# Local attention and a gated MLP on one core: the output product of the last batch by seven block products

## The chip, the core and the metric

One NeuronCore of a Trainium2 chip runs the whole program. Its engines are TensorE (PE in the rows, with its weight loads as PEld), VectorE (DVE), ScalarE (ACT), GpSimd (POOL) and SyncE (SP, which here issues DMAs). They run side by side, each in the order of its own instruction queue, and wait for each other by semaphores. The metric is device time in microseconds. Every time here is of the program of one launch.

## The reference

Four batches of 768 tokens, 8 heads of 64. Attention looks at chunks of 32 tokens, each with 16 tokens to its left, 8 to its right and 8 memory tokens. Its output x (768 x 512 per batch) goes through a gated MLP; the products are what TensorE spends its time on:

```python
h = np.maximum(x @ w_in, 0.0)                       # 512 -> 1024
u, v = h[..., :512], h[..., 512:]
v_n = (v - mean(v)) / np.sqrt(var(v) + 1e-06)
v_s = np.einsum('ts,bsd->btd', w_spatial, v_n) + b_spatial[None, :, None]
gated = u * v_s
out = (gated @ w_out).astype(np.float32)            # 512 -> 512
```

## The kernel before

Every fp32 operand of the MLP is kept as two rounded parts, a high one (an ACT copy) and a low one (value minus high part, on DVE or POOL), and a product is three matmuls: high by high, low by high, high by low. A group of matmuls sums into one PSUM tile `f`. A block is 128 rows by 512, 384 or 256 columns.

The program runs over the batches. Per batch there are `ffn_v` (v, six groups of 12 matmuls of 512 columns), `ffn_u` (u, eight groups of 12 of 384), the spatial product (`spatial`, L1061 and after) and the output product (`ffn_o`). The attention of the next batch is laid between the matmuls of the present one: for each block of 128 tokens one burst of 64 small matmuls (scores of one block, values of the block before), and between two bursts a softmax chain over DVE, ACT and POOL.

In the last batch there is no attention left to lay between. There the spatial product is already done by Strassen: `strassen` makes seven products of half size, P2, P1, P6, P5, P3, P7, P4, of 18 matmuls of 384 columns each (L1236). Their right-hand sides are sums of blocks of v (`forms`) and of w_spatial (`w_forms`, L1201 for the sums, L1210 and L1212 for the two parts). After a product DVE adds the PSUM tile to the bias, or to what was kept (L1294); a finished quarter is multiplied by u on POOL (L1275) and split again into its parts g (ACT L1280, DVE L1284). Then `ffn_o` makes the output: six tiles of 128 tokens, each 12 matmuls of 512 columns (four blocks of g by three). The last tile is made as two halves of 256 columns. ACT copies each tile out (L1399) and SP stores it (L1401).

What runs when is not in the order of the code. `Plan` collects all operations with their engine, a cost, what they read and write and a rank; `order` then sets every engine's queue by simulating them, and the instructions are issued in that order. POOL and DVE share a way to SBUF, and the plan keeps them apart there: while any POOL operation runs, no DVE operation marked `port` is placed, and the other way round. `ORDER` is a table of corrections by operation number (a shift of the rank, a bonus in waiting, an engine), which here covers operations 0 to 429 only:

```python
if e == "POOL" or e == "DVE" and ops[n][11]:
    late = max(late, free["port"])
```

Of the kernel before, what the change touches and what calls it, by code (L numbers as in the profile page):

```python
# [8 lines left out]
F32 = mybir.dt.float32  # L9
# [111 lines left out]
}  # L121
# [86 lines left out]
class Plan:  # L208
# [13 lines left out]
    def op(self, eng, us, fn, r=(), w=(), rank=0.0, moves=0.0, tail=0.0, after=None, count=0, port=False):  # L222
        n = len(self.ops)
        wait = 0.0
# [25 lines left out]
        return n  # L250

    def order(self):
# [20 lines left out]
        while len(out) < len(ops):  # L273
            best = None
            for e, ns in waiting.items():
                pick, lead = None, None
                for n in ns:
# [15 lines left out]
                    if e == "POOL" or e == "DVE" and ops[n][11]:  # L293
                        late = max(late, free["port"])
# [23 lines left out]
            if e == "POOL" or e == "DVE" and port:  # L318
                free["port"] = t + us
# [41 lines left out]
def tile_chunked_attention_gmlp(  # L361
# [508 lines left out]
    def place(i, rank):  # L870
        j = i - 1

        def go(e, c):
            if c == 0:
                alloc("xs", j, [P, T, UC, CH], F32)
# [339 lines left out]

    def strassen(b):
# [8 lines left out]
        def product(name, form, piece_, banks, first, reads=((), ())):  # L1225
            begun = []
            prev = t_.get("product", last["u"])
            for j in range(2):
                cols = slice(j * P, (j + 1) * P)
                for s in range(NQ):  # L1230
                    def go(j=j, s=s, cols=cols):
# [9 lines left out]
                               *(x for f in ("B11", "B21") for y in range(NQ) for x in piece_keys(f, y) if name == "P2" and s == 0)],  # L1241
                            w=[("f", banks[j], name, s)], rank=1e4 + seq[0], tail=0.25, after=prev, count=6)
# [18 lines left out]
        def out_of(hf, d, rank, start_, more=()):  # L1261
# [10 lines left out]

            def mult():
                a = t_["st", s_]
                nc.gpsimd.tensor_tensor(a, a, t_["u", i], op=ALU.mult)  # L1275

            def high():
                if not g_place(i):
                    t_["g", i] = alloc("big", big, [P, 1024], U32).bitcast(F32R).rearrange("p (s n) -> p s n", s=2)
                nc.scalar.copy(g_of(i)[0][:, 0:HT], t_["st", s_])  # L1280

            def low():
                h, l_ = g_of(i)
                nc.vector.tensor_tensor(l_[:, 0:HT], t_["st", s_], h[:, 0:HT].bitcast(F32), op=ALU.subtract)  # L1284
            op("POOL", 1.05, mult, r=[("u", i)], w=[k_], rank=rank)
            op("ACT", act(HT), high, r=[k_], w=[gh], rank=rank)
            op("DVE", dve(HT), low, r=[k_, gh], w=[gl], rank=rank)
# [32 lines left out]
        last[b, 0] = last[b, 1]  # L1320
        for hf in range(2):
            for t in range(HU):
                ffn_o(b, hf, t, 2 if hf == 1 and t == HU - 1 else 1)
# [18 lines left out]
    def spatial(b, hf, d):  # L1342
# [33 lines left out]
        op("POOL", 1.05, mult, r=[("u", i)], w=[k_], rank=rank)  # L1376
        op("ACT", act(HT), high, r=[k_], w=[("big", big, "h")], rank=rank)
        op("DVE", dve(HT), low, r=[k_, ("big", big, "h")], w=[("big", big, "l")], rank=rank)
# [26 lines left out]
    def from_f64(name, dst, src_, rank, load_rank, over=(), pieces=1, gate=None, stage=None):  # L1405
# [58 lines left out]
        def convert():  # L1464
# [11 lines left out]
            op("POOL", 1.27, add, r=[(big[0], big, "r")], w=[zk], rank=rank + LATER)  # L1476
# [17 lines left out]
    def w_sp_part(t, rank, load_rank):  # L1494
# [13 lines left out]
        op("POOL", pool_(S), low, r=[("big", big), ("wsp", t, "h")], w=[wl_key(t) + ("l",), *(early_keys() if t < 3 else ())], rank=rank)  # L1508
# [22 lines left out]
    for b in range(B):  # L1531
# [17 lines left out]
        if b == B - 1:  # L1549
            w_forms()  # L1550
            strassen(b)
# [50 lines left out]
```

## Time and profile before

| | us |
|---|---|
| median of 3 runs | 373.35 (373.32 to 374.25) |
| the profiled execution, as a whole | 372.5 |
| its span, first to last instruction | 370.7 |
| PE busy | 353.7 (95%) |
| DVE, ACT, POOL busy | 226.4, 259.5, 162.9 |
| the seven spatial products of the last batch | 328.66 to 350.69 |
| the output product of the last batch | 350.69 to 367.37 |

An engine's busy time counts matmuls with modelled, overlapping ends, so a stretch of matmuls is read by the distance from one start to the next. The output product ends 3.3 us before the span does; what lies between is the last copy and the last store.

### The profile page before, as it was taken

To read this page: it belongs to the slowest core of one execution; us is meant where nothing else is said; L and a number is where in the kernel's file an instruction comes from. 1 tells how busy PE (TensorE), PEld (TensorE's weight loads), DVE (VectorE), ACT (ScalarE), POOL (GpSimd) and SP (SyncE) were. 2 spreads that over 40 slices of the span, in tenths; PEclk is the share of its full clock that TensorE was granted. 3 is DMA by queue.
4 is the path that set the end of the run, shared out by engine and by line. 5 is a ranking of instruction groups with operands and counts; after the bars stand their busy time and mean duration, and the time that the engine had idled before them with its cause. 6 is when DMAs were issued, how large, how long until landed. Compare 5 with 4: busy or idle time off the path is not lost.

```text
span 370.7 us, 11379 instructions
## 1 busy us (share of the span) xinstructions
PE 353.7 (95%) x4710; PEld 316.7 (85%) x4710; DVE 226.4 (61%) x445; ACT 259.5 (70%) x678; POOL 162.9 (44%) x255
## 2 busy tenths in 40 slices
PE   3659999999999999999999999999999999999996
PEld 3437988999899898899899889899899889899985
DVE  2797878977556376647448476555538477784610
ACT  5688898863596697887886787967886876551222
POOL 3776674653454241432543330543533563724600
PEclk9998999999999999999999999999999999999999
DMA  6999847881105271061025272071030230200013
GB/s 219 288 317 243 294 110 205 235 256 54 55 34 175 93 166 51 3 224 51 2 88 175 87 143 76 6 226 33 20 131 2 87 127 3 87 0 2 0 58 113
DMA packets 30108, 42.08 MB, mean 114 GB/s; under 512 B 5288, under 2 KB 23400, under 8 KB 30056
## 3 DMA queue, kind: packets, MB, share of 16 engines
q1 hardware_dynamic: 29832, 41.26, 36.4%
q8 instruction: 37, 0.61, 0.7%
q14 instruction: 15, 0.12, 0.1%
q10 hardware_dynamic: 224, 0.08, 0.1%
HBM read 35.05 MB, written 6.29 MB: 112 GB/s over the span
## 4 chain that ended last, share of the span: by engine, by line
PE 91%; DMA 4%; DVE 2%; ACT 1%; issue 1%; SPq 0%
PE f L1061 75%; PE sx L789 8%; PE f L1236 6%; DMA big<-in_moe_w_in_dram 4%; PE xt L1005 1%; PE pt L978 1%; SPq L512 0%; ACT vmain L737 0%; DVE win_l L1463 0%; DVE stage_z L1445 0%; PE f L789 0%; DVE st L1451 0%; DVE xs L859 0%; DVE p L907 0%; ACT st L1435 0%
## 5 line engine op out<-in xcount | busy, mean ns | idle before, releaser
L1061 PE MATMUL f<-x,win_h 128*128 128x384 f32 x256 | 72.7, 342 | 0.0
L879 ACT COPY xs<-sx 32x128 f32<-32x128 f32 x240 | 61.5, 256 | 3.4 <-PE sx L789 0.6
L1061 PE MATMUL f<-win_h,x 128*128 128x512 f32 x192 | 63.3, 411 | 0.0
L1061 PE MATMUL f<-wout,big 128*128 128x512 f32 x252 | 62.7, 392 | 0.0
L1061 PEld LDWEIGHTS f<-wout,big 128*128 128x128 f32 x252 | 46.7, 188 | 8.8
L1061 PEld LDWEIGHTS f<-x,win_h 128*128 128x128 f32 x256 | 47.0, 188 | 1.4
L1061 PE MATMUL f<-x,win_l 128*128 128x384 f32 x128 | 43.3, 338 | 0.0
L1366 POOL TENSOR_TENSOR st<-st,u 128x384 f32<-128x384 f32 x24 | 25.4, 1065 | 39.0 <-DVE st L1362 34.4
L1061 PEld LDWEIGHTS f<-win_h,x 128*128 128x128 f32 x192 | 35.7, 192 | 7.5 <-DVE x L1015 0.9
L486 ACT COPY pT<-p 32x128 f32<-32x128 f32 x128 | 37.9, 296 | 2.5 <-POOL p L958 1.0
L1061 PE MATMUL f<-win_l,x 128*128 128x512 f32 x96 | 38.7, 403 | 0.0
L1061 PE MATMUL f<-wsp_h,vb 128*128 128x384 f32 x144 | 37.5, 341 | 0.0
L958 POOL TENSOR_TENSOR p<-p,rec 128x512 f32<-128x512 f32 x15 | 16.0, 1064 | 48.0 <-DVE rec L935 48.0
L1061 PE MATMUL f<-wsp_h,va 128*128 128x384 f32 x144 | 36.9, 337 | 0.0
L486 POOL COPY pT<-p 32x128 f32<-32x128 f32 x112 | 33.7, 301 | 5.0
L1107 POOL TENSOR_TENSOR rstd<-ve,mhalf 128x1 f32<-128x1 f32 x24 | 15.9, 664 | 38.3 <-DVE ve L1103 20.5
L922 ACT ACTIVATE p<-p 128x512 f32<-128x512 f32 x24 | 15.1, 629 | 21.4 <-DVE p L907 21.3
L1399 ACT COPY st<-f 128x512 f32<-128x512 f32 (+1 forms) x25 | 13.9, 571 | 20.4 <-PE f L1061 17.2
L1061 PEld LDWEIGHTS f<-wsp_h,va 128*128 128x128 f32 x144 | 26.1, 188 | 0.6
L1061 PEld LDWEIGHTS f<-wsp_h,vb 128*128 128x128 f32 x144 | 25.7, 188 | 1.0
L1099 DVE BATCH_NORM_STATS2 stats<-st 128x6 f32<-128x512 f32 x24 | 16.6, 691 | 14.8 <-ACT st L1095 14.6
L1061 PEld LDWEIGHTS f<-x,win_l 128*128 128x128 f32 x128 | 24.1, 188 | 0.9
(164 smaller groups left out, 721.5 us busy)
## 6 DMA issues: line engine op xcount, KB each, us to landing
out_dram<-st SPq DMA_DIRECT2D x23, 256.0 KB
k<-in_k_dram SPq DMA_DIRECT2D x7, 800.0 KB
q<-in_q_dram SPq DMA_DIRECT2D x7, 768.0 KB
vmain<-in_v_dram SPq DMA_DIRECT2D x38, 128.0 KB
big<-in_moe_w_spatial_dram SPq DMA_DIRECT2D x12, 384.0 KB
vmain<-in_v_dram SPq DMA_DIRECT2D x37, 96.0 KB
big<-in_moe_w_in_dram SPq DMA_DIRECT2D x4, 512.0 KB
stage_w<-in_moe_w_in_dram SPq DMA_DIRECT2D x4, 512.0 KB
```

The costliest lines, as they stand in the source:

```text
L486: return (nc.scalar.copy if e == "ACT" else nc.gpsimd.tensor_copy)(o, a).ins
L789: nc.tensor.matmul(o, w_, m, start=start, stop=True, skip_group_check=True)
L879: last_ = (nc.scalar.copy if e == "ACT" else nc.vector.tensor_copy)(o, a).ins
L922: nc.scalar.activation(p3, p3, AF.Exp, scale=scale)
L958: (nc.vector if e == "DVE" else nc.gpsimd).tensor_tensor(p3, p3, rec, op=ALU.mult)
L978: nc.tensor.transpose(a[:, t], p[:, t], ident)
L1061: return [nc.tensor.matmul(o, ll if x == 1 else lh, rl if x == 2 else rh, start=x == j == 0, stop=j == len(pairs) - 1 and x == (single[-1] ...
L1099: nc.vector.bn_stats(stats, t_["st", s])
L1107: nc.gpsimd.tensor_tensor(a, t_["ve", i], mhalf, op=ALU.pow)
L1236: return [nc.tensor.matmul(o, l_ if x == 1 else h, w_[1] if x == 2 else w_[0], start=first and s == x == 0, stop=s == NQ - 1 and x == 2, s ...
L1366: nc.gpsimd.tensor_tensor(a, a, t_["u", i], op=ALU.mult)
L1399: nc.scalar.copy(alloc("st", s_, [P, N], F32), t_["f", n])
```

## The change

The output product of the last batch is done by Strassen as well. `strassen_o` takes the place of the calls of `ffn_o` there: out = g w_out in blocks of 384 tokens by 256 columns, seven products P4, P1, P6, P5, P7, P2, P3 of 18 matmuls of 256 columns (three tiles of 128 tokens, two blocks of g, three matmuls). The sums on the weight's side are made by `wout_sums` and split by `wout_forms`; those on g's side (S1 to S4) are made and split in `out_of`, where two of the four first-half blocks need no parts any more. Products are added to what earlier ones left in PSUM or kept in SBUF (`keep`, `give`), and each quarter of the output is stored in three pieces of 128 x 256.

Three more things change. In the spatial product the last third of P2 and P1 is moved behind the first two thirds of both. From operation 430 on only marked operations of two tensors exclude each other on POOL and DVE; single-tensor POOL copies no longer hold DVE back in the plan, in any batch from about the first output product on. And `ORDER` gets 423 entries for operations 1236 to 1764, the last batch.

```diff
+    1236: (-220.6, 6, ''), 1237: (-206.9, 0, ''), 1238: (-214.5, 0, ''), 1239: (15.2, 0, ''),
...
-TSUB = {"DVE": 0.37, "POOL": 0.72}
-TLOW = {"DVE": 0.37, "POOL": 0.72}
-TSUB2 = {"DVE": 0.69, "POOL": 1.32}
+TSUB = {"DVE": 0.37}
+TLOW = {"DVE": 0.37}
+TSUB2 = {"DVE": 0.69}
-SLOW = {"POOL": 1.05}
+SLOW = {"DVE": 0.55, "POOL": 1.05}
+EXACT = 430
...
+        port = port or pair and n >= EXACT
...
+    def holds(self, e, n):
+        return self.ops[n][11] if n >= EXACT else e == "POOL" or e == "DVE" and self.ops[n][11]
...
+    def wout_sums():
...
+                op(FSUM, 0, full, r=[("wout", d, x) for x in "hl"], w=[key_(m), key_(m + 1)], rank=FRANK,
+                   after=last["out", B - 2], port=True)
+            for o, x, y in ((0, 1, 0), (1, 3, 1), (3, 3, 0), (2, 2, 3)):
+                op(TSUB, 0, lambda e, s=s, o=o, x=x, y=y: vec(e).tensor_tensor(
+                    o_f(s)[:, o], o_f(s)[:, x], o_f(s)[:, y], op=ALU.subtract),
...
-        product("P2", "A12", "B21", Bk, True)
-        product("P1", "A11", "B11", A, True)
+        for steps in (range(NQ - 1), range(NQ - 1, NQ)):
+            product("P2", "A12", "B21", Bk, True, steps=steps)
+            product("P1", "A11", "B11", A, True, steps=steps)
...
+        wout_forms(("token", "P1"))
         product("P6", "S2", "T2", A, False, [[("rd", A[j], "P1")] for j in range(2)])
...
+            if hf == 0 and part == 0:
+                g_split()
+            elif hf == 0:
+                sub("S1", s0, s0, s1, [two_key(1)], two_key(0), ALU.add)
+                s_split("S1", s0, two_key(0))
+            elif part == 1:
+                g_split()
+                sub("S2", s0, s0, full, [fk], two_key(0))
+                sub("S3", s1, full, s1, [fk], two_key(1))
+                s_split("S2", s0, two_key(0))
+                s_split("S3", s1, two_key(1))
+            else:
+                g_split()
+                sub("S4", full, full, s0, [two_key(0)], fk)
+                s_split("S4", full, fk)
...
-            for t in range(HU):
-                ffn_o(b, hf, t, 2 if hf == 1 and t == HU - 1 else 1)
+        strassen_o(b)
...
+        product("P4", lambda k: g_(0, k), lambda k: f_("T4", k), "V", True)
+        keep("P4", "V", 0)
+        product("P1", lambda k: g_(1, 2 + k), lambda k: w_(2 + k, 0), "X", True)
+        keep("P1", "X", 1)
+        product("P6", lambda k: s_("S2", k), lambda k: f_("T2", k), "X", False, "P1")
+        for t in range(HU):
+            after("P6", "X", t, "DVE", lambda t=t: nc.vector.tensor_tensor(hold(0, t), bank("X", t), hold(0, t), op=ALU.add),
+                  w=[("vb", ("o", 0), t)])
+        product("P5", lambda k: s_("S1", k), lambda k: f_("T1", k), "X", False, "P6")
+        keep("P5", "X", 2)
+        product("P7", lambda k: s_("S3", k), lambda k: f_("T3", k), "Y", True)
+        give("P7", "Y", 2, 0, 1, "22")
+        give("P7", "Y", 0, 0, 0, "21")
+        product("P2", lambda k: g_(1, k), lambda k: w_(k, 0), "W", True)
+        give("P2", "W", 1, 1, 0, "11")
+        product("P3", lambda k: s_("S4", k), lambda k: w_(k, 1), "X", False, "P5")
...
```

Three places show how the queues change; the numbers behind the names tell the tiles apart. The first is PE at the passage from spatial P1 to P6, before: `f_5221` and `f_5239` are the two tiles of P1, which P6 goes on with, `va` holds parts of v, `x` and `q` the operands of P6:

```order
L1236 MATMUL f_5221<-w1_914,va_5158 128x384
L1236 MATMUL f_5239<-wsp_h_813,va_4915 128x384 [waits Activation_49]
L1236 MATMUL f_5239<-wsp_h_813,va_4915 128x384
L1236 MATMUL f_5239<-w0_1086,va_4915 128x384
L1236 MATMUL f_5239<-wsp_h_813,va_4991 128x384 x2
L1236 MATMUL f_5239<-w0_1265,va_4991 128x384
L1236 MATMUL f_5239<-wsp_h_813,va_5158 128x384 x2
L1236 MATMUL f_5239<-w1_914,va_5158 128x384
L1236 MATMUL f_5221<-x_5023,q_4983 128x384 [waits DVE_49]
```

The same passage now, where `f_5201` and `f_5213` are the tiles of P2, `f_5223` and `f_5233` those of P1:

```order
L1400 MATMUL f_5201<-wsp_h_813,va_5061 128x384 x2
L1400 MATMUL f_5201<-w1_954,va_5061 128x384
L1400 MATMUL f_5213<-wsp_h_813,va_5061 128x384 x2
L1400 MATMUL f_5213<-w1_954,va_5061 128x384
L1400 MATMUL f_5223<-wsp_h_813,va_5061 128x384 x2
L1400 MATMUL f_5223<-w1_914,va_5061 128x384
L1400 MATMUL f_5233<-wsp_h_813,va_5061 128x384 x2
L1400 MATMUL f_5233<-w1_914,va_5061 128x384
L1400 MATMUL f_5223<-x_5116,q_4972 128x384 [waits DVE_49,Activation_49]
```

Between the last matmul into P1's first tile and the first of P6, which adds to that tile, there were nine matmuls and are now three. The second place is DVE at the last additions of the spatial product, before; `st<-f,va` is the addition (L1294) and `win_l` the low part of a block of g (L1284):

```order
L1294 TENSOR_TENSOR st_5376<-f_5327,va_5268 128x384 [waits DVE_49,PE_49]
L1284 TENSOR_TENSOR win_l_116<-st_5362,win_h_115 128x384 [waits Activation_49]
L1294 TENSOR_TENSOR st_5391<-f_5343,va_5268 128x384 [waits DVE_49,PE_49]
L1284 TENSOR_TENSOR win_l_116<-st_5376,win_h_115 128x384 [waits Activation_49]
L1284 TENSOR_TENSOR win_l_116<-st_5391,win_h_115 128x384 [waits Activation_49]
```

And now; the additions are L1499, the sums on g's side L1475, low parts L1458 (`x_5116` those of S1 and S2, `win_l` those of g and S3), and L1610 is the first addition of the output's P6:

```order
L1499 TENSOR_TENSOR st_5403<-f_5357,va_5288 128x384 [waits PE_49]
L1458 TENSOR_TENSOR win_l_116<-st_5376,win_h_115 128x384 [waits Activation_49]
L1475 TENSOR_TENSOR big_5276<-big_5276,st_5376 128x384 [waits DVE_49]
L1458 TENSOR_TENSOR x_5116<-big_5286,x_5116 128x384 [waits Activation_49]
L1458 TENSOR_TENSOR win_l_116<-st_5390,win_h_115 128x384 [waits Activation_49]
L1475 TENSOR_TENSOR big_5286<-big_5286,st_5390 128x384 [waits DVE_49]
L1458 TENSOR_TENSOR x_5116<-big_5276,x_5116 128x384 [waits Activation_49]
L1475 TENSOR_TENSOR big_5276<-st_5376,big_5276 128x384
L1475 TENSOR_TENSOR big_5286<-st_5390,big_5286 128x384
L1458 TENSOR_TENSOR x_5116<-big_5286,x_5116 128x384 [waits Activation_49]
L1458 TENSOR_TENSOR win_l_116<-big_5276,win_h_115 128x384 [waits Activation_49]
L1610 TENSOR_TENSOR vb_5429<-sx_5444,vb_5429 128x256 [waits PE_49]
```

Behind the addition for the first tile of spatial P4 there stood four operations to the end of the program; now eight stand between it and the second low part of S2 (the last `x_5116`), and the addition for P4's second tile (`f_5372`) comes only after the output's P6 has begun. The third place is PE at the output's P1 and P6 now, which wait for these parts:

```order
L1568 MATMUL sx_5444<-wout_835,win_h_115 128x256 [waits PE_49,Activation_49]
L1568 MATMUL sx_5444<-wout_835,win_l_116 128x256 [waits DVE_49]
L1568 MATMUL sx_5444<-wout_835,win_h_115 128x256
L1568 MATMUL sx_5444<-wout_835,win_h_115 128x256 [waits Activation_49]
L1568 MATMUL sx_5444<-wout_835,win_l_116 128x256 [waits DVE_49]
...
L1568 MATMUL sx_5444<-wsp_h_813,x_5116 128x256 [waits Activation_49]
L1568 MATMUL sx_5444<-wsp_h_813,x_5116 128x256 [waits DVE_49]
L1568 MATMUL sx_5444<-w0_1265,x_5116 128x256
L1568 MATMUL sx_5444<-wsp_h_813,x_5116 128x256
L1568 MATMUL sx_5444<-wsp_h_813,x_5116 128x256 [waits DVE_49]
```

Each of the two products waits for the two low parts of its blocks on DVE, the second one four matmuls after its first.

## Rows read from the trace of the kernel before

**Rows 1.** The chain that ended last: start, us, engine, what, line.
```profile
99.81 1.41 PE sx L789 x89
...
269.61 1.41 PE sx L789 x89
...
280.80 1.41 PE sx L789 x91
...
350.85 15.85 PE f L1061 x77
...
367.61 0.37 ACT st L1399
```
**Rows 2.** Busy time of each engine by stretch, with PE clock and DMA share.
```profile
29.97:294.00 264.03, 264.03 (x3819) 237.23 (x3819) 165.00 (x321) 205.02 (x561) 117.20 (x201) 0.99 0.38 112
294.00:328.00 34.00, 34.00 (x231) 30.57 (x230) 24.39 (x55) 21.57 (x59) 16.06 (x19) 1.00 0.24 82
328.66:350.69 22.03, 22.03 (x128) 22.03 (x128) 14.34 (x28) 6.33 (x14) 10.34 (x11) 1.00 0.00 1
350.69:367.37 16.68, 16.68 (x85) 14.07 (x84) 2.04 (x4) 4.24 (x8) 1.96 (x2) 1.00 0.18 66
```
**Rows 3.** PE in order of time, end of the output product: start, us, instruction.
```profile
366.07 0.28 PE L1061 MATMUL f<-wout,win_l 128*128 128x256 f32 x1
...
367.25 0.28 PE L1061 MATMUL f<-wout,win_h 128*128 128x256 f32 x1
```
**Rows 4.** PE in order of time, end of spatial P1's first tile.
```profile
333.20 0.34 PE L1236 MATMUL f<-w,va 128*128 128x384 f32 x1
...
334.95 0.51 PE L1236 MATMUL f<-x,q 128*128 128x384 f32 x2
```
**Rows 5.** DVE in order of time, the spatial product; in brackets what ended an idle time.
```profile
333.58 0.56 DVE L1294 TENSOR_TENSOR st<-f,st 128x384 f32<-128x384 f32 x1 [0.52 <-PE f L1236]
...
345.25 1.42 DVE L1284 TENSOR_TENSOR big<-st,big 128x384 fp32r<-128x384 f32 x1
...
349.79 0.55 DVE L1294 TENSOR_TENSOR st<-f,va 128x384 f32<-128x384 f32 x1
350.26 0.55 DVE L1284 TENSOR_TENSOR win_l<-st,win_h 128x384 fp32r<-128x384 f32 x1
```
**Rows 6.** POOL in order of time, the spatial product.
```profile
345.23 1.01 POOL L1275 TENSOR_TENSOR st<-st,u 128x384 f32<-128x384 f32 x1 [0.57 <-DVE st L1294]
...
350.48 2.17 POOL L1275 TENSOR_TENSOR st<-st,u 128x384 f32<-128x384 f32 x2 [1.03 <-DVE st L1294]
```
**Rows 7.** DVE by line and shape, 280 to 332 us: count, busy us, mean ns.
```profile
L1201 DVE TENSOR_TENSOR big<-big 128x384 f32<-128x384 f32 x10 | 5.5, 553 | 1.2 <-DMA big<-in_moe_w_spatial_dram 1.1
...
L1160 DVE TENSOR_TENSOR p<-st,p 128x256 fp32r<-128x256 f32 x1 | 0.4, 420 | 0.0
```
**Rows 8.** Sum over 280 to 332 us of each engine's busy time.
```profile
sum 52.00, PE 52.00 PEld 46.72 DVE 37.23 ACT 35.05 POOL 22.48; mean PE 4.00 PEld 3.59 DVE 2.86 ACT 2.70 POOL 1.73
```
**Rows 9.** POOL copies, beside a DVE operation and alone.
```profile
95.54 1.56 POOL L486 COPY pT<-p 32x128 f32<-32x128 f32 x4
...
265.90 1.28 POOL L486 COPY pT<-p 32x128 f32<-32x128 f32 x4
```
**Rows 10.** DVE beside those copies, and the last step before a burst.
```profile
96.06 0.56 DVE L1373 TENSOR_TENSOR big<-st,big 128x384 fp32r<-128x384 f32 x1 [1.14 <-ACT big L1369]
...
268.35 0.70 DVE L985 STREAM_TRANSPOSE p<-pT 128x512 f32<-128x512 f32 x1
```
**Rows 11.** The end: SP's issues of the last three stores, in order of time.
```profile
366.44 1.90 SPq L1401 DMA_DIRECT2D out_dram<-st  x3
```
**Rows 12.** Stretches of the end, columns as in rows 2.
```profile
368.00:368.50 0.50, 0.00 (x0) 0.00 (x0) 0.00 (x0) 0.00 (x0) 0.00 (x0) 1.00 0.66 228
...
369.00:369.50 0.50, 0.00 (x0) 0.00 (x0) 0.00 (x0) 0.00 (x0) 0.00 (x0) 1.00 0.49 168
```

More of the change, by code (lines that the diff above doesn't have):

```diff
@@ L292, in order @@
                     late = max(t, free[e])
-                    if e == "POOL" or e == "DVE" and ops[n][11]:
+                    if self.holds(e, n):
                         late = max(late, free["port"])
@@ L317, in order @@
             free[e] = t + us
-            if e == "POOL" or e == "DVE" and port:
+            if self.holds(e, n):
                 free["port"] = t + us
@@ new lines, in wout_forms @@
+    def wout_forms(token):
+        for form, m in (("T4", 2), ("T1", 0), ("T2", 3), ("T3", 1)):
+            for s in range(2):
+                h, l_ = o_t_keys(form, s)
+                k_ = ("vm", NU + s, m)
+                op("ACT", act(DQ), lambda form=form, s=s, m=m: nc.scalar.copy(o_t(form, s)[0], o_f(s)[:, m]),
+                   r=[k_, token], w=[h], rank=FRANK)
+                op(TLOW, 0, lambda e, form=form, s=s, m=m: vec(e).tensor_tensor(
+                    o_t(form, s)[1], o_f(s)[:, m], o_t(form, s)[0].bitcast(F32), op=ALU.subtract),
+                   r=[k_, h, token], w=[l_], rank=FRANK, port=True)
@@ L1223, in strassen, with product @@
         tok = [slice(hf * HT, (hf + 1) * HT) for hf in range(2)]
-        def product(name, form, piece_, banks, first, reads=((), ())):
+        def product(name, form, piece_, banks, first, reads=((), ()), steps=range(NQ)):
             begun = []
@@ L1229, in product @@
                 cols = slice(j * P, (j + 1) * P)
-                for s in range(NQ):
+                for s in steps:
                     def go(j=j, s=s, cols=cols):
@@ L1271, in out_of @@
                 f(lambda: t_["st", s_], k_)
-            def mult():
[L1274 to L1284, printed above, removed]
@@ L1285, in out_of, with two, two_key @@
-            op("POOL", 1.05, mult, r=[("u", i)], w=[k_], rank=rank)
-            op("ACT", act(HT), high, r=[k_], w=[gh], rank=rank)
-            op("DVE", dve(HT), low, r=[k_, gh], w=[gl], rank=rank)
+            j, part = d % 2, d // 2
+            def two(m, j=j):
+                if ("o", j) not in t_:
+                    t_["o", j] = alloc("big", ("big", ("o", j)), [P, 1024], U32).bitcast(F32)
+                return t_["o", j][:, m * HT:(m + 1) * HT]
+            def two_key(m, j=j):
+                return ("big", ("big", ("o", j)), m)
@@ new lines, in full, with split @@
+            def full(part=part, two=two, s_=s_):
+                return t_["st", s_] if hf else two(part)
+            fk = k_ if hf else two_key(part)
+            def mult():
+                nc.gpsimd.tensor_tensor(full(), t_["st", s_], t_["u", i], op=ALU.mult)
+            def split(src_, key_, place, hk, lk, form=None):
+                rank_ = rank + LATER_S.get(form, 0.0)
+                op("ACT", act(HT), lambda: nc.scalar.copy(place()[0], src_()), r=[key_], w=[hk], rank=rank_)
+                op(GLOW, 0, lambda e: vec(e).tensor_tensor(place()[1], src_(), place()[0].bitcast(F32), op=ALU.subtract),
+                   r=[key_, hk], w=[lk], rank=rank_, port=True)
@@ new lines, in s_split, with keys, g_split, place @@
+            def s_split(form, src_, key_):
+                def keys():
+                    a = O_S[form]
+                    return [("win", a[1] + j, 1, x) for x in "hl"] if a[0] == "win" else [("x", 8, a[2] + j, x) for x in "hl"]
+                split(src_, key_, lambda: o_s(form, j), *keys(), form)
+            def g_split():
+                def place():
+                    if not g_place(i) and ("g", i) not in t_:
+                        t_["g", i] = alloc("big", big, [P, 1024], U32).bitcast(F32R).rearrange("p (s n) -> p s n", s=2)
+                    return [x[:, 0:HT] for x in g_of(i)]
+                split(full, fk, place, gh, gl)
```

144 lines of the change are left out of this document (134 added, 10 removed), and 77 rows, old and new, of the table ORDER.

## The prediction

> **What bounds the kernel now.** I read the chain of waits first, then the busy time by stretch, then the order of time at the places that the change touches. The chain is to be seen as a chain of TensorE: from 29 us on it is matmuls only, and after them one ACT copy of 0.37 us and the last store [rows 1]. The stretches say the same from the other side: PE is busy in 264.03 of 264.03 us, in 34.00 of 34.00, and to the last hundredth in both products of the last batch, at a granted clock of 1.00 (the 2.4 GHz level) in the last three stretches [rows 2]. DVE, ACT and POOL have room in each of them. So a microsecond of matmuls removed is a microsecond won, as long as nothing else makes PE wait; and since PE waits for nothing today, another order on the other engines can only lose.
>
> The sum is made against the profiled execution: 372.5 us, of which the span is 370.7 and 1.8 lie around it. The median of the three runs is 373.35, 0.85 above it; a difference found on the one is carried to the other.
>
> **Matmuls removed and added.** The output product of the last batch takes 16.68 us [rows 2]: 60 matmuls of 512 columns and 24 of 256. All of it goes. In its place come seven products of 18 matmuls of 256 columns, 126 in all. That shape is in the trace: the starts at 366.07 and 367.25 are ten matmuls apart, each with a weight load of its own, so one takes 0.118 us [rows 3]. 126 x 0.118 = 14.87 us. The difference is 16.68 - 14.87 = 1.81 us. (By columns it would be 32256 against 36864, an eighth; a matmul of half the width costs a little more than half.)
>
> **The passage from spatial P1 to P6.** P6 adds to the tile that P1 leaves, so its first matmul waits until DVE has read P1's first tile. Before, nine matmuls lay between; the addition began 0.38 us after the start of the last matmul into that tile (333.20 to 333.58), took 0.56, and was over at 334.14 while P6 began at 334.95 [rows 4, 5]. Now three lie between. A spatial matmul takes 22.03 / 126 = 0.175 us [rows 2], so P6 could start 4 x 0.175 = 0.70 after that last matmul, and the tile is free at 0.38 + 0.56 = 0.94; with 0.04 for the signal back (DVE began 0.04 after the modelled end, 333.20 + 0.34, [rows 4, 5]) PE stands for 0.28 us. DVE is free at that time: before this addition it has the two of P2, 0.47 apart when they follow each other (349.79 to 350.26 [rows 5]), and their tiles are ready 1.05 and 0.52 earlier. The split gives nothing back, since P2 does not wait today. Queued behind the addition on DVE are a low part (L1324) and one of the new weight forms (L1376) and then P1's second addition; P6 needs that one 1.58 us later, and two operations of 0.47 fit.
>
> **New work before the last batch's spatial product.** On DVE there come three double sums of w_out (512 wide; a 384-wide one takes 0.553, so about 0.7), seven of the eight differences (0.42 each), seven low parts of w_spatial's sums that were POOL's (0.55) and three quarter-width steps that were POOL's (0.42); three of L1201's sums go to POOL (0.553) [rows 7]. 2.1 + 2.9 + 3.9 + 1.3 - 1.7 = 8.5 us. Between 280 and 332 us DVE is idle for 52 - 37.23 = 14.8 us [rows 8]. I cost it at nothing, hidden behind 52 us of matmuls that read none of it until P2; if the cover fails, the low parts of v that P2 reads come late and PE waits by as much. The split of P2 and P1 helps here: the last pair of v's blocks is needed only 24 matmuls, 4.2 us, after P2's start.
>
> **New work beside the two products.** The sixteen operations for the two parts of T1 to T4 (ACT 0.4, DVE 0.42 each) fall into the spatial product, where ACT is busy for 6.33 and DVE for 14.34 of 22.03 us [rows 2], and cost nothing. The sums S1 to S4 are the tight place. With PE 0.28 us later, DVE's addition for P4's first tile can start at 349.60 (its last matmul starts at 349.40 - 0.175, and 0.38 after that), and nine operations of 0.47 follow up to the second low part of S2: the fourth of them, the second low part of g, ends at 350.07 + 3 x 0.47 + 0.55 = 352.03, the ninth at 354.38. The output product starts at 350.97. Its P1 needs the one at 350.97 + 22 x 0.118 = 353.57, its P6 the other at 350.97 + 40 x 0.118 = 355.69. That leaves 1.5 and 1.3 us. POOL multiplies by u at this time, 1.0 to 1.1 us each (350.48, two in 2.17) [rows 6], and when both engines take two tensors from SBUF one stands still: at 345.23 a multiplication of 1.01 and a DVE operation of 0.55 met, and DVE took 1.42 [rows 5, 6]. One such meeting is to be expected (the multiplication of P4's first tile) and takes up to 0.87; 0.4 us remain. So: nothing, but with little to spare. The later ones, g's parts of P4 and S4, are needed by the output's P2 and P3, 90 and 108 matmuls after its start, and have over 2 us.
>
> **The end.** Twelve stores of 128 KB take the place of five of 256 and two of 128, and none can start before the output's P7. Two bounds: DMA moved 228 GB/s in a stretch at a share of 0.66, so 345 at full share, and 168 in the stretch of the last store alone [rows 12]. 1.57 MB then take 4.6 or 9.3 us. The first store can start at about 360.8, so the last bytes would be there at 365.4, before the last copy, or at 370.1 against 369.5 in the trace. I take the first, since the stretch with the lower rate held a single store, which could not fill it. SP needs 1.90 / 3 = 0.63 us per issue at most, part of it waiting [rows 11]; twelve issues have 5.6 us from 360.8 and the last three come at the pace of PE. From the last matmul's start to the last copy's and to the span's end it stays 0.36 and 3.1 us.
>
> **Sum.** -1.81 + 0.28 = -1.53: the profiled execution goes from 372.5 to 371.0, the median from 373.35 to 371.8.
>
> **A rule of the skill on the new rule of the plan.** The plan now lets POOL's copies run beside DVE's two-tensor operations. Trace: four copies of pT took 1.28 us alone and 1.56 beside a DVE operation, which itself took its usual 0.56 [rows 9, 10]; so they do meet, and here the copy lost 0.28. The Trainium skill, "SBUF — State Buffer", section "Who interferes with whom", says that a DVE instruction with two SBUF inputs contends with a GpSimd instruction that reads SBUF and that the later one blocks fully. The trace agrees, and by that rule the plan's new premise is wrong for copies. For the time it matters only where the loss outgrows the slack, which is the third rival.
>
> **Rivals.**
>
> (1) The chain of S sums comes late: two meetings on DVE and POOL instead of one, and ACT's high parts in between, put the second low part of S2 at 354.38 + 2 x 0.87 = 356.1, 0.4 late, and PE's wait shifts nothing later into cover: P7's S3 and the additions behind it have the same queue. With half a microsecond lost at two of the seven products the time is 372.8. For it: nine operations in one queue with 0.4 to spare. Against: two meetings need POOL to have two multiplications ready inside 4 us, and the second waits for an addition that now stands behind these nine.
>
> (2) DVE's 8.5 us do not fit into its 14.8 because its work waits for ACT and POOL half the time: P2 starts a microsecond late, 372.8 as well. For: between 294 and 328 DVE and POOL together are busy for 24.39 + 16.06 of 34 us already [rows 2], and two-tensor work on the one stops the other. Against: the split of P2.
>
> (3) Slower than before: the meetings of POOL's copies with DVE, allowed in the plan from operation 430 on, stretch the softmax chain of each burst. 14 bursts lie between 99.81 and 280.80 [rows 1]. The one at 269.61 has its last step over at 268.35 + 0.70 = 269.05 [rows 1, 10], 0.56 in hand. Up to two meetings of 0.28 per burst cost nothing; with three, PE stands 0.28 at each burst, 14 x 0.28 = 3.9 us, and the time is 375.7. It decides from the third meeting on one chain. For: rows 9. Against: copies and DVE meet in the old order too, and PE has no wait there.
>
> (4) The end is bound by the stores, by the lower rate above: 0.6 us later, 372.4.
>
> **Chances and range.** Forecast 0.62, own range 371.2 to 372.2 (nothing lost at the passage and 0.3 less spent on matmuls, or 0.4 more lost than I count); (1) 0.15, (2) 0.07, (3) 0.10, (4) 0.06. The range reaches over (1), (2) and (4) with some room for both together: 371.2 to 373.5; it leaves out (3) and a gain of more than 2.1. Within 0.3% means 1.12 us on this time, about what a measurement can tell from no change, so the bound for faster is 372.23: the forecast lies 0.4 inside it, rivals (1), (2) and (4) just outside. Faster 0.64 (the forecast and a part of the small rivals), same 0.26, slower 0.10.
>
> **What would show it.** In the profile after: 126 matmuls of 256 columns starting 0.118 apart; a gap of about 0.3 between the last matmul of spatial P1 and the first of P6, with DVE L1499 as what ended it; no gap at the output's P1 and P6; the last copy 0.36 after the last matmul's start; PE without idle time at the bursts. It would be wrong if PE's starts in the output product spread over more than 15.3 us, if bursts after 100 us begin behind an idle PE, or if the last store begins long after the last copy.

## The result, and the profile of the changed kernel

The changed kernel takes 377.96 us in the median of six runs (376.33 to 378.28), the kernel before 373.59 in six beside them. The ratio on record is 1.0089, interval 1.0065 to 1.0112 (the quotient of the two medians is 1.0117): slower, where 371.8 was predicted. The profiled execution took 376.33 us, 1.6 under the median of its kernel; its span is 374.5, 3.8 above that of before. So the profile accounts for 3.8 us. Two executions further on, one with X in three tiles and the profiled one of the kernel with P1's last step first, took 859.5 and 857.91 us and stand in no ratio.

Where they are, by the stretches of the last batch. Columns as in [rows 2]; first the spatial product, then the output product up to the last matmul's end.

```profile
330.02:353.10 23.08, 22.69 (x127) 21.85 (x127) 18.46 (x37) 9.11 (x22) 11.57 (x11) 1.00 0.00 1
353.10:371.30 18.20, 16.15 (x127) 15.21 (x126) 13.15 (x27) 7.33 (x19) 3.93 (x4) 1.00 0.19 66
```

The spatial product begins at 330.02 instead of 328.66 (+1.36) and takes 23.08 instead of 22.03 us (+1.05). The output product, from its start to that of its last matmul and 0.12 more, takes 18.18 instead of 16.68 (+1.50, where -1.81 was predicted). From the last matmul's start to the end it is 0.11 less. 1.36 + 1.05 + 1.50 - 0.11 = 3.80. The clock is at 1.00 (2.4 GHz) in both, as before; what is new is PE's idle time, which [rows 2] did not have. What PE waited for after 100 us (us in total, times, longest):

```profile
PE sx L1568 <- ACT vb L1596: 0.9, 2, 0.5
PE sx L1568 <- DVE vb L1610: 0.6, 1, 0.6
PE sx L1568 <- ACT st L1621: 0.5, 1, 0.5
PE f L1400 <- DVE st L1499: 0.4, 2, 0.2
PE f L1173 <- DVE x L1127: 0.2, 1, 0.2
```

**The output product.** All four of its waits are on tile `sx`, none on the `f` tiles of P4, P7 and P2. PE in the middle of P1 (start, us, instruction; in brackets the idle time and what ended it), and ACT beside it:

```profile
356.18 0.28 PE L1568 MATMUL sx<-wout,win_h 128*128 128x256 f32 x1
356.92 0.39 PE L1568 MATMUL sx<-wout,win_h 128*128 128x256 f32 x1 [0.46 <-ACT vb L1596]
```

```profile
356.50 0.37 ACT L1596 COPY vb<-sx 128x256 f32<-128x256 f32 x1 [0.38 <-PE sx L1568]
```

The matmul at 356.18 writes t1, the second half of `sx`. ACT's copy reads t0, the first half, whose last matmul started at 355.82, three before this one; yet it begins at 356.50, just after that matmul into t1 has ended (356.18 + 0.28), and PE's next matmul into t1 begins just after the copy has ended (356.50 + 0.37 = 356.87). PE and reader alternate on two halves that have nothing to do with each other. The gap is 0.74 from start to start where 0.118 is usual. At the start of P5 the same happens through DVE; its rows, and PE's:

```profile
359.73 0.42 DVE L1610 TENSOR_TENSOR vb<-sx,vb 128x256 f32<-128x256 f32 x1 [0.78 <-PE sx L1568]
360.07 0.55 DVE L1499 TENSOR_TENSOR st<-f,va 128x384 f32<-128x384 f32 x1
360.54 0.42 DVE L1610 TENSOR_TENSOR vb<-sx,vb 128x256 f32<-128x256 f32 x1
```

```profile
361.00 0.50 PE L1568 MATMUL sx<-wsp_h,x 128*128 128x256 f32 x2 [0.61 <-DVE vb L1610]
```

P6's addition of t0 waits for P6's matmuls on t1 (to 359.69), an L1499 (an addition of the spatial product) stands between, and P5's first matmul on t0 (361.00) waits for the addition of t1, over at 360.96. The other two gaps are at the second block of t1 in P5 (362.80) and in P3 (370.09), of the same kind as P1's; P6 has none. The four gaps are 0.740, 0.888, 0.741 and 0.797: 2.69 us above four pitches of 0.118. The matmul behind each takes 0.224 to the next start instead of 0.118, 0.42 in all.

**The passage.** PE around the end of P1's first tile, which answers to [rows 4], and DVE and POOL, which answer to [rows 5, 6]:

```profile
336.13 0.34 PE L1400 MATMUL f<-w,va 128*128 128x384 f32 x1
336.69 1.83 PE L1400 MATMUL f<-x,q 128*128 128x384 f32 x9 [0.22 <-DVE st L1499]
338.68 0.62 PE L1400 MATMUL f<-x,q 128*128 128x384 f32 x2 [0.17 <-DVE st L1499]
```

```profile
335.98 0.56 DVE L1499 TENSOR_TENSOR st<-f,st 128x384 f32<-128x384 f32 x1
336.46 0.55 DVE L1324 TENSOR_TENSOR x<-big,x 128x384 fp32r<-128x384 f32 x1
336.92 1.24 DVE L1376 TENSOR_TENSOR w<-vmain,wsp_h 128x256 fp32r<-128x256 f32 x1
338.09 0.54 DVE L1499 TENSOR_TENSOR st<-f,st 128x384 f32<-128x384 f32 x1
```

```profile
336.62 1.26 POOL L1453 TENSOR_TENSOR big<-st,u 128x384 f32<-128x384 f32 x1 [1.00 <-DVE st L1499]
```

The first gap is the predicted one: 0.56 from start to start, 0.38 above the pitch (the usual distance from one start to the next), where 0.28 was worked out. The second was not predicted. The low part L1376 met POOL's multiplication, took 1.24 instead of 0.42, and P1's second addition came 0.8 late. A smaller delay, 0.14 with the matmul behind it, is at P3's start (343.3).

**Before the last batch's products.** Two new stalls: one at the burst at 128 us (0.45 from start to start, where the other bursts behind a matmul of 512 columns have 0.32 to 0.33), one at 308 us.

```profile
127.91 0.40 PE L1173 MATMUL f<-win_l,x 128*128 128x512 f32 x1
128.36 0.79 PE L901 MATMUL sx<-k,q 64*32 64x64 f32 x60
...
307.39 0.43 PE L1173 MATMUL f<-win_h,x 128*128 128x512 f32 x1
308.05 0.50 PE L1173 MATMUL f<-win_h,x 128*128 128x512 f32 x1 [0.23 <-DVE x L1127]
```

**What held.** In the chain that the prediction counted, the S sums lose one meeting, 1.38 us for a 0.55 us operation (row below, which answers to the 345.25 of [rows 5]; another, 1.37 us at 349.52, lies before the chain), and no PE gap follows from it. The stores (SP, last three in 1.78, against [rows 11]) cost nothing.

```profile
352.79 1.38 DVE L1475 TENSOR_TENSOR big<-big,st 128x384 f32<-128x384 f32 x1
...
370.43 1.78 SPq L1588 DMA_DIRECT2D out_dram<-st  x3
```

### The profile page after: what moved, and what is told of

Same layout as the page of the kernel before. It is cut to its first block, busy times and chain, and to the rows that moved or that the text cites. A ratio compares the mean times of both kernels' runs of the same rounds, so it can differ in the third digit from the quotient of the medians.

```text
span 374.5 us, 11535 instructions
## 1 busy us (share of the span) xinstructions
PE 355.4 (95%) x4752; PEld 318.0 (85%) x4752; DVE 246.3 (66%) x494; ACT 267.1 (71%) x697; POOL 165.0 (44%) x252
## 4 chain that ended last, share of the span: by engine, by line
PE 87%; DMA 5%; DVE 4%; ACT 2%; issue 1%; SPq 0%; ACTq 0%; DVEq 0%
PE f L1173 67%; PE sx L901 8%; PE f L1400 5%; PE sx L1568 2%; PE f L1568 2%; DMA vmain<-in_v_dram 1%; DMA big<-in_moe_w_spatial_dram 1%; DMA q<-in_q_dram 1%; PE xt L1117 1%; DMA v<-in_mem_v_dram 1%; PE pt L1090 1%; PE xt L1568 1%; DVE win_l L1762 0%; SPq L624 0%; DVE stage_z L1744 0%
## 5 line engine op out<-in xcount | busy, mean ns | idle before, releaser
L1173 PE MATMUL f<-win_h,x 128*128 128x512 f32 x192 | 64.1, 414 | 0.2 <-DVE x L1127 0.2
L1173 PE MATMUL f<-wout,big 128*128 128x512 f32 x216 | 55.9, 394 | 0.0
L1173 PEld LDWEIGHTS f<-wout,big 128*128 128x128 f32 x216 | 39.8, 188 | 7.0 <-DVE big L1672 0.2
L598 POOL COPY pT<-p 32x128 f32<-32x128 f32 x112 | 35.1, 313 | 5.2
L1661 DVE TENSOR_TENSOR st<-f,bias 128x384 f32<-128x384 f32 x24 | 13.3, 556 | 23.2 <-PE f L1173 23.0
L901 PEld LDWEIGHTS sx<-k,q 64*32 64x32 f32 x1536 | 17.5, 110 | 9.4 <-issue 4.1
```

What stands on the lines that cost most here:

```text
L598: return (nc.scalar.copy if e == "ACT" else nc.gpsimd.tensor_copy)(o, a).ins
L901: nc.tensor.matmul(o, w_, m, start=start, stop=True, skip_group_check=True)
L1173: return [nc.tensor.matmul(o, ll if x == 1 else lh, rl if x == 2 else rh, start=x == j == 0, stop=j == len(pairs) - 1 and x == (single[-1] ...
L1661: nc.vector.tensor_tensor(alloc("st", s_, [P, HT], F32), t_["f", n], bias[:, tok], op=ALU.add)
```

## The experiments

Theory: the output product lost its gain because t0 and t1 of set X (the accumulators of P1, P6, P5 and P3) are halves of one PSUM tile, and the program waits by tile. Rival: ACT and DVE are late by themselves. The remaining 2.4 us are taken apart afterwards. The ratios of each experiment are to the kernel before, run beside it.

### X in three tiles of its own

```diff
-            return ("f", sets[x][t]) if x != "X" else ("sx", "o") if t < 2 else ("xt", "o")
+            return ("f", sets[x][t]) if x != "X" else (("pt", "sx", "xt")[t], "o")
...
-            return t_[k_][:, t * 512:t * 512 + N] if k_[0] == "sx" else t_[k_][:, 0:N]
+            return t_[k_][:, 0:N]
```

> The changed kernel with one thing changed: the three tiles of the bank set X of the last batch's output product lie in three PSUM tiles of their own (pt, sx, xt), where the first two were the two halves of one tile sx. Theory (the wait is on the shared tile: tensor engine, ScalarE and VectorE wait for each other's half): the four gaps in front of products on X (0.74, 0.89, 0.74 and 0.80 us) go, the output product falls from 18.2 us to 15.0 to 15.6, and the whole by 2.6 to 3.1 us: profiled execution about 373.5, ratio to the kernel before about 1.001. Rival (the readers on ScalarE and VectorE are late by themselves, queued behind other work): the gaps stay within 0.2 us each, the output product stays above 17.5 us and the ratio at about 1.009.

Measured: 374.59 us, ratio 1.0029 (1.0003 to 1.0055). The theory holds. The spatial product and then the output product, columns as above:

```profile
331.54:354.62 23.08, 22.67 (x127) 21.82 (x127) 18.45 (x37) 9.09 (x22) 11.57 (x11) 1.00 0.00 1
354.62:369.60 14.98, 14.98 (x127) 14.89 (x126) 12.28 (x27) 7.35 (x19) 4.26 (x4) 1.00 0.21 73
```

PE is busy in all of the output product. Its 126 starts lie within 14.81 us, where the changed kernel needs 18.05: 3.24 us for one tile. The two programs issue the same operations in the same order on every engine, so the order is not what made the difference. ACT's copy of t0 now runs while PE writes t1 (its row, and PE's beside it):

```profile
357.66 0.38 ACT L1596 COPY vb<-pt 128x256 f32<-128x256 f32 x1
```

```profile
357.46 0.28 PE L1568 MATMUL sx<-wout,win_h 128*128 128x256 f32 x1
```

The Trainium skill, "Perfetto Trace Analysis", section "Matmuls", advises to let independent matmul groups rotate through different PSUM banks, so that the evacuation of one overlaps the next one's matmuls. The rows here name tiles and not banks: t0 and t1 lay 512 float32 columns apart in one tile and did not overlap; as tiles of their own they did. So in this program independent groups have to be different tiles as well.

### The shared tile moved to t1 and t2

```diff
-            return ("f", sets[x][t]) if x != "X" else ("sx", "o") if t < 2 else ("xt", "o")
+            return ("f", sets[x][t]) if x != "X" else (("xt", "sx", "sx")[t], "o")
...
-            return t_[k_][:, t * 512:t * 512 + N] if k_[0] == "sx" else t_[k_][:, 0:N]
+            return t_[k_][:, (t - 1) * 512:(t - 1) * 512 + N] if k_[0] == "sx" else t_[k_][:, 0:N]
```

> The changed kernel, with the shared tile of bank set X holding its tiles t1 and t2, and t0 alone. Theory (the wait belongs to the shared tile): the gaps move with it: those at the second block of t1 in P1, P5 and P3 (0.74, 0.74 and 0.80 us) now stand at the second block of t2, six matmuls later, and the one at the start of P5 (0.89 us) at the first block of its t1; the output product stays at about 18 us. Rival (the readers on ScalarE and VectorE are late): the gaps stay at t1's second block and at P5's first.

One run, 376.68 us. PE's three gaps in the output product:

```profile
359.52 0.28 PE L1568 MATMUL xt<-w,x 128*128 128x256 f32 x1
360.24 0.50 PE L1568 MATMUL sx<-wsp_h,x 128*128 128x256 f32 x2 [0.44 <-ACT vb L1596]
...
362.36 0.28 PE L1568 MATMUL xt<-w,x 128*128 128x256 f32 x1
362.78 0.51 PE L1568 MATMUL sx<-wsp_h,x 128*128 128x256 f32 x2
...
370.37 0.29 PE L1568 MATMUL sx<-wout,win_h 128*128 128x256 f32 x1
371.17 0.38 PE L1568 MATMUL sx<-wout,win_h 128*128 128x256 f32 x1 [0.52 <-ACT st L1621]
```

Every gap is at a matmul into `sx`, none at t0, which has `xt` alone, and none at t1's second block: the rival is out. Of the four places two came as expected (P3's at t2, 0.80; P5's at t1's first block, though 0.42 and not 0.89). P1's moved to the first block of P6's t1 instead, and P5's second went. The output product's starts spread over 16.85 us, not 18.

### P2 and P1 whole again

```diff
-        for steps in (range(NQ - 1), range(NQ - 1, NQ)):
+        for steps in (range(NQ),):
...
-                               *(x for f in ("B11", "B21") for y in range(NQ) for x in piece_keys(f, y) if name == "P2" and s == 0 and y < NQ - 1)],
+                               *(x for f in ("B11", "B21") for y in range(NQ) for x in piece_keys(f, y) if name == "P2" and s == 0)],
```

> The changed kernel with the last batch's spatial products P2 and P1 whole again, one after the other, and with P2 waiting for all its operands at its start, as in the kernel before. Theory (the split brings P1's tiles to an end so close to P6 that P6 waits for VectorE): the gaps at 336.1 (0.56 us) and 338.2 (0.33 us) go and with them the slow matmul behind each, the spatial product falls from 23.1 us to 22.1 to 22.4, the whole by 0.7 to 1.0 us, ratio to the kernel before about 1.006 to 1.007. Rival (the gaps come from VectorE's queue, whatever the order): a gap of like size stays at P6, and P2's start waits for the last sum on top: no gain, ratio 1.009 or more.

Measured: 385.39 us, ratio 1.0317 (1.0278 to 1.0356). The first part of the expectation came true: both gaps of the passage are gone and PE is busy throughout the spatial product (first row below: 21.85 of 21.85 us). The time did not follow, for a reason that neither theory had: in the order that the planner gave, two of the differences of w_out (DVE L1365, last row) stand on DVE behind the S sums, so T4's first part came late and PE stood in front of the output product.

```profile
330.60:352.45 21.85, 21.85 (x127) 21.80 (x126) 16.26 (x32) 8.33 (x20) 12.31 (x11) 1.00 0.00 1
...
361.00:363.00 2.00, 2.00 (x11) 2.00 (x11) 1.97 (x4) 1.16 (x3) 1.03 (x1) 0.50 0.00 0
...
365.30:371.00 5.70, 4.72 (x37) 4.30 (x36) 1.27 (x3) 1.12 (x3) 0.00 (x0) 1.00 0.02 3
```

```profile
359.62 0.58 PE L1568 MATMUL f<-wsp_h,big 128*128 128x256 f32 x1 [6.84 <-ACT wsp_h L1374]
```

```profile
357.46 1.54 DVE L1365 TENSOR_TENSOR vmain<-vmain 128x256 f32<-128x256 f32 x2
```

So the gaps hang on the split, and the run says nothing of their price. Why the planner placed the two there was not looked into; that the corrections of `ORDER`, made for the changed kernel, no longer fit is a guess.

### P1's last step first

```diff
-            product("P2", "A12", "B21", Bk, True, steps=steps)
-            product("P1", "A11", "B11", A, True, steps=steps)
+            pair = [("P2", "A12", "B21", Bk, True), ("P1", "A11", "B11", A, True)]
+            for p in pair if steps[0] == 0 else pair[::-1]:
+                product(*p, steps=steps)
...
-            out_of(0, j, 45 + 1e-3 * seq[0], plus(Bk[j], "P2", 0),
-                   [plus(A[j], "P1", None, lambda i=i: t_["st", ("st", "g", i)])])
+            out_of(0, j, 45 + 1e-3 * seq[0], plus(A[j], "P1", 0),
+                   [plus(Bk[j], "P2", None, lambda i=i: t_["st", ("st", "g", i)])])
...
```

> The run with X in three tiles, and besides: of the split spatial products the last step of P1 is issued ahead of the last step of P2, and the sum of the two starts with P1 (P1 + bias, then + P2). So nine matmuls lie between the end of P1's first tile and P6's first matmul on it, where three did. Theory (the distance is too short for VectorE's two additions): the gaps at the passage to P6 (0.56 and 0.53 us) go, the spatial product falls by 0.9 to 1.1 us, time about 373.6, ratio to the kernel before 1.000. Rival (P6 waits because VectorE's queue holds the weights' subtractions in front of the additions, whatever the order): at least one gap of 0.3 us or more stays, gain under 0.5 us, ratio 1.002 or more.

Measured: 374.61 us, ratio 1.0005 (0.9981 to 1.0029). The interval holds the theory's 1.000 and the rival's 1.002, so the times do not decide. The profile is not used here; the gaps are shown by the kernel with the later rule, below, which has the same products.

### The new rule of the plan

First the rule alone in the kernel before:

```diff
+EXACT = 430
...
+    def holds(self, e, n):
+        return self.ops[n][11] if n >= EXACT else e == "POOL" or e == "DVE" and self.ops[n][11]
```

> The kernel before with only the planner's new rule: from operation 430 on GpSimd's multiplications and subtractions exclude VectorE's two-tensor operations in the plan, its other operations no longer do. Nothing else of the change is in it. Theory of the prediction (the new order costs nothing): 373.2 to 374.0 us, ratio 0.999 to 1.002. Rival (the orders that the rule gives are worse: copies of GpSimd fall on VectorE's work and bursts wait): the spatial product begins 1 us or more later, ratio 1.003 or more.

Measured: 374.28 us, ratio 1.0015 (0.9986 to 1.0045): no verdict from the times. The profile shows one thing of it: the stall at the burst, with nothing else of the change in the kernel.

```profile
127.81 0.40 PE L1066 MATMUL f<-win_l,x 128*128 128x512 f32 x1
128.29 0.79 PE L794 MATMUL sx<-k,q 64*32 64x64 f32 x60
```

The burst begins 0.48 us after the last matmul before it, and no other burst after 100 us does; 0.32 is usual here, so the stall is 0.16. Then the kernel with P1's last step first ("the run before" in what was expected), with the rule from operation 1050 on:

```diff
-EXACT = 430
+EXACT = 1050
```

> The run before with the planner's new rule from operation 1050 on, not from 430: up to about 280 us the instructions stand in the order of the kernel before, the last batch keeps its order. Theory (the new rule's order of the earlier batches costs the stall at a burst of attention at 128 us): the gap of 0.45 us there goes, nothing else changes, time about 0.4 us under that of the run before, ratio about 0.999. Rival (the stall has another cause): it stays, ratio 1.000.

Measured: 373.61 us, ratio 1.0002 (0.9982 to 1.0023). The stall at the burst is gone, as expected, but it was 0.16 us and not the 0.45 that the expectation took for it, and the times cannot tell so little. The gaps at P6 are gone too, so the distance between P1's end and P6's start was too short. But one appears further on, at P3 (PE, and DVE in front of it):

```profile
344.96 0.34 PE L1400 MATMUL f<-win_l,vb 128*128 128x384 f32 x1
345.97 0.62 PE L1400 MATMUL f<-win_h,vb 128*128 128x384 f32 x2 [0.68 <-DVE va L1499]
```

```profile
343.20 1.58 DVE L1376 TENSOR_TENSOR w<-vmain,wsp_h 128x256 fp32r<-128x256 f32 x2 [0.47 <-ACT wsp_h L1374]
344.70 0.41 DVE L1376 TENSOR_TENSOR x<-vmain,x 128x256 fp32r<-128x256 f32 x1
345.04 0.41 DVE L1365 TENSOR_TENSOR vmain<-vmain 128x256 f32<-128x256 f32 x1
345.37 1.01 DVE L1499 TENSOR_TENSOR va<-f,bias 128x384 f32<-128x384 f32 x2
```

Four operations on w_out's forms stand in front of P5's addition. The spatial product still takes 22.98 us. So the expected gain did not come: the work in DVE's queue is the same, and PE now waits at a later product that needs the queue.

### The low parts of w_out's forms on GpSimd

```diff
+TFORM = {"DVE": 0.37, "POOL": 0.72}
...
-                op(TLOW, 0, lambda e, form=form, s=s, m=m: vec(e).tensor_tensor(
+                op(TFORM, 0, lambda e, form=form, s=s, m=m: vec(e).tensor_tensor(
```

(four of the eight set to POOL in the table, the others to DVE.)

> The run with P1's last step first and the new rule from operation 1050 on, and besides: four of the eight low parts of the output weights' forms (those of T1, T2 and T3 that VectorE took between 341 and 347 us) are GpSimd's. Theory (what is left of the spatial product's stall is VectorE's queue: at 345 us the tensor engine waits 1.0 us for P5's addition, which stands behind 2.4 us of these low parts): the gap goes, the spatial product takes 22.0 to 22.3 us in place of 23.0, time about 372.7, ratio to the kernel before about 0.998. Rival (GpSimd's copies of this work collide with VectorE's two-tensor operations and the loss comes back): gaps of 0.5 us or more stay or appear in the output product, ratio 1.000 or more.

Measured: 372.57 us, ratio 0.9962 (0.9942 to 0.9982): faster than before, and than the changed kernel. That is 1.1 us under the 373.71 of before, of the 1.8 that the fewer matmuls give. The list of waits has none of PE after 100 us; spatial and output product:

```profile
330.28:352.42 22.14, 22.14 (x127) 21.94 (x127) 17.45 (x34) 9.23 (x22) 13.80 (x14) 1.00 0.00 1
352.42:367.40 14.98, 14.98 (x127) 14.89 (x126) 12.41 (x27) 7.31 (x19) 4.32 (x4) 1.00 0.21 73
```

The same edit, with five low parts on POOL, in the kernel with X in three tiles alone tells distance and queue apart:

> The run with X in three tiles alone (P2's last step ahead of P1's, as in the changed kernel), with five of the eight low parts on GpSimd. If the short distance between P1's end and P6's start makes the first gap by itself, it stays at 0.5 to 0.6 us (only additions stand in front of it on VectorE), while the second, behind a low part of 1.24 us, goes or halves: spatial product 22.5 to 22.8 us, ratio about 1.000 to 1.002. If the queue of low parts makes both, both go: spatial product 22.1 us, ratio 0.999.

Measured: 374.30 us, ratio 1.0018 (0.9995 to 1.0041); spatial product 22.79 us. PE and DVE at the first gap:

```profile
337.09 0.34 PE L1401 MATMUL f<-w,va 128*128 128x384 f32 x1
337.65 0.58 PE L1401 MATMUL f<-x,q 128*128 128x384 f32 x2 [0.22 <-DVE st L1500]
```

```profile
336.95 0.56 DVE L1500 TENSOR_TENSOR st<-f,st 128x384 f32<-128x384 f32 x1
337.42 0.55 DVE L1325 TENSOR_TENSOR x<-big,x 128x384 fp32r<-128x384 f32 x1
```

The first gap stays at 0.56 and the second, which had the 1.24 us low part in front, is gone. So the split makes the first gap by itself. The second takes both: in the kernel with the rule from 1050 on, the same low part of 1.24 us stands in front of P1's second addition and nine matmuls of distance cover it. A gap of 0.36 remains at P3.

### The sums of w_out cut short

```diff
-                    vec(e).tensor_tensor(o_f(s)[:, m:m + 2], ...
+                    vec(e).tensor_tensor(o_f(s)[:, m:m + 2, 0:8], ...
```

> The changed kernel with the sums of the output weights (12 operations on VectorE and GpSimd ahead of the spatial product) cut to 8 of their 256 columns; the output of the last batch is then not the reference's. Theory of the prediction (this work lies in idle time): the spatial product still begins at 329.5 to 330.1 us and the time stays that of the changed kernel, ratio 1.009. Rival (these sums push VectorE's queue and through it the sums of the spatial weights and the activations): the spatial product begins at 328.6 to 329.0 us, the time falls by 1.0 to 1.4 us, ratio about 1.005 to 1.006.

Measured: 377.18 us, ratio 1.0091 (1.0059 to 1.0124): the theory's number. The stall at 308 us was gone, which put the question whether the sums cause it; so the same edit once more, in the kernel with the rule from operation 1050 on ("the run before"):

> The run before with the sums of the output weights cut to 8 of their 256 columns (the last batch's output is then not the reference's). Theory (these sums lengthen VectorE's queue, and the stall of 0.43 us at 308 us hangs on it): the gap at 308 us goes and the time falls by another 0.4 to 0.6 us, ratio about 0.998. Rival (the stall comes from the landing of the spatial weights alone): it stays, same time as the run before.

Measured: 373.16 us, ratio 0.9984 (0.9965 to 1.0004), not to be told from 1.0002. The stall was there, at 0.12 us above the pitch. What it goes by is in the chain of waits of the changed kernel (start, us, engine, what), which leaves PE between 295.77 and 308.05:

```profile
295.77 5.46 DMA big<-in_moe_w_spatial_dram
308.05 22.14 PE f L1173 x113
```

```profile
301.32 0.56 DVE L1313 TENSOR_TENSOR big<-big 128x384 f32<-128x384 f32 x1 [1.99 <-DMA big<-in_moe_w_spatial_dram]
```

DVE's first sum of w_spatial stands at the head of its queue and waits for the first load of these weights, and what PE needs at 308 stands behind it. From the load's issue to DVE's start it is 5.55 us here. The five profiles with whole sums and the rule from 430 give, for this time and PE's gap at 308 (above 0.23): 5.17 and some 0.05, 5.45 and 0.33, 5.55 and 0.43, 5.58 and 0.46, 5.61 and 0.49; the two with the rule from 1050 on 5.16 and some 0.05, 5.64 and 0.49. (The 0.05 are worked out: two matmuls took 0.62 where 0.465 is usual, and about 0.105 of that is the slower matmul behind a stall.) With short sums it is 5.48 and 0.12, and 3.93 and none. So the stall goes with the load's landing, which differs from profile to profile; by one profile the sums add some 0.24 to it (0.12 where the others give 0.36). This was found by lining up profiles, not by an experiment that holds the landing fixed.

## Why the prediction was wrong

The forecast was 1.53 us less, the profile has 3.80 more. Of the 5.3 between them 3.3 are in the output product, 1.4 before the spatial product and 0.8 in it; the end gives 0.1 back.

- **The matmuls: right.** 126 x 0.118 = 14.87 us was predicted; where nothing stalls, the starts spread over 14.81 and PE is busy for 14.98. The gain of 1.8 us is real, and each run with X in three tiles has it.
- **The step that failed: that the output product would take 126 pitches of 0.118 and nothing else.** The prediction followed the waits of P1 and P6 for their operands (g and the S sums), and these came in time. It put waits for the accumulators of set X at nothing without a word, in P1 as in P5 and P3, where three of the four gaps are: it did not ask what a wait is set on. `bank` cuts t0 and t1 from one tile `sx`, and a read of the one half and a write of the other wait for each other. This costs 3.24 us, all of the gain of 1.8 and 1.4 more; its own sign of being wrong, starts spread over more than 15.3 us, came with 18.05. The planner has the same blind spot: its keys name product, t and block, so in its order halves are free of each other, and it gave the same order with X in three tiles. The output product of before used `f` tiles alone, so its rows could not show it; the code could.
- **The passage: mechanism right for the first tile, size wrong.** 0.28 was forecast for P6's first tile, 0.38 measured. The addition ran as counted (335.98 to 336.54), but PE began 0.15 after it and not 0.04; its first matmul now waits for two engines, and a semaphore instruction of 51 ns stands in front of it at 336.58, which may be a part of this (not tested). "Two operations of 0.47 fit" in front of the second tile's addition was wrong: from start to start they took 0.46 and 1.17. The price of a meeting with POOL stood in [rows 5, 6] and was charged at the S sums only. With the slow matmul behind each gap, and the 0.14 at P3, the spatial product lost 1.05.
- **The work before the last batch: too low.** It was costed at nothing, and the spatial product began 1.36 late. The sums are worth about 0.24 us when the load of w_spatial lands late, and the changed kernel's stall at 308 us was 0.43, and 0.11 on the matmul behind it. Rival (2), P2 a microsecond late, is near by its number only: P2 itself follows the matmul before it without a gap (329.85 to 330.02).
- **The chain of S sums and the end: right.** One meeting, 1.38 us as the row of before had it, and no wait from it. The stores hide, and the tail is 0.11 shorter. So rivals (1) and (4) are out.
- **Rival (3), the only slower one, had the sign and not the mechanism.** It wanted 0.28 at each of 14 bursts; one burst stalled, by 0.13 us in the changed kernel and 0.16 with the rule alone, and in the three profiles with the rule from 1050 on none does. The prediction took its rows to agree that the later operation blocks fully; they agree in kind only: the copies lost 0.28 us beside a DVE operation of 0.56 [rows 9, 10].
- **Open.** Of the 1.36 us before the spatial product, 0.3 are there already at the burst at 55 us, in code that the change does not touch (55.43 against 55.72; over all profiles up to 57.25). With the 0.54 at 308 us and the 0.13 at 128, some 0.4 of the 1.36 are left without a place. And the six timed runs of the changed kernel lie 1.6 above its profile in the median; those with X in three tiles do not (374.59 against 374.65 profiled). The profile of the changed kernel is one that came early to the burst at 55 us (55.72), that with X in three tiles a late one (57.23); this 1.5 would be nearly all of the difference, but no late profile of the changed kernel is on record.

## What to carry to other kernels

Before counting a product as free of waits, look up what its accumulator is cut from: in this program two halves of one tile were one thing to wait on, though 512 columns apart, and a planner that tracks halves won't see it. When an order is tight, charge the known price of a meeting between VectorE and GpSimd at each place where PE waits on VectorE's queue, not only at the one that looks tightest. And test a gain by removing one suspected wait at a time: here the matmuls had won 1.8 us all along, and the 3.2 us of one tile hid them.

## What the hardware showed besides

Each stall cost more than its gap: the matmul behind it took 0.105 to 0.11 us longer to the next start at each of three widths (0.224 for 0.118 at 256 columns, 0.28 for 0.175 at 384, 0.34 for 0.23 at 512), and behind the passage's first gap 0.075 (0.25 for 0.175). Gaps of up to 0.9 us left the granted clock at 1.00; after the wait of 6.84 us it was 0.50 (1.2 GHz) from 361 to 363 us, where a matmul of 256 columns took about 0.21 us, and from 365.3 on it was 1.00 again. The Trainium skill, "TensorE: Matmul & The Clock Gate", section "What's actually happening", says that idle time takes the clock to half rate; the trace agrees.
